# New hand-set first steps, fewer warming products and a new written order in a clustered-attention and two-MLP kernel

## The chip, the cores and the metric

The kernel runs on one core of a Trainium2 chip. The metric is the device time of one execution in microseconds (us); a comparison uses the median of several executions. The core has five engines that work side by side: TensorE (PE, matrix products; its weight loads are shown as PEld), VectorE (DVE), ScalarE (ACT), GpSimd (POOL) and SyncE (SP, which here only issues DMA transfers).

## What is computed

Attention with 2 batches, 8 heads, 768 tokens and 64 channels per head, in which a query sees only the keys of its own cluster; then two MLPs on the 1536 tokens of 512 channels.

```
q_assign = argmax(q_n @ c_n.T);  k_assign = argmax(k_n @ c_n.T)   # 16 centroids per head
mask   = q_assign[:, None] == k_assign[None, :]
attn   = softmax(where(mask, q @ k.T / 8, -1e9));  x = attn @ v
h      = x @ w_in                                   # 512 -> 2048
x      = where(h > 0, h, exp(min(h, 0)) - 1) @ w_out
out    = ((x @ w_a) * (x @ w_b)) @ w_out2           # 512 -> 1536 -> 512
```

Weights come as 64-bit floats. Results are float32; every factor of a product is split into a high and a low part, so that one product becomes several.

## The kernel before, in words

The work is cut into 16 heads (`g`), taken two at a time as 8 pairs (`j`). A head's scores are 6 tiles (`t`) of 128 queries by 768 keys; three tiles make a half (`f`).

No loop orders the work. A long string, `ORDER`, lists some 2300 words, and the last loop of the kernel calls one small function for each. A word such as `th:0.1.1.0/pt=0` is a name, its numbers, and the buffer to take. Every engine runs its own instructions in the order of the words, and waits where an operand or a buffer is not ready. Where a function has a choice of engine, the last number makes it: 0 is DVE, 1 is ACT, 2 is POOL (for loads, 0 is SP's queue and 1 ACT's).

The words of the attention, by what they do:

- Loads: `lk` keys and `lp` queries of a pair, `lq` one head's queries twice (two transfers), `vl` a quarter of V, `wl` a piece of a weight; `kbd`, `ohd` are copies by DMA between tiles.
- Clusters: `c0` to `c4` prepare the centroids (a square root by ACT in `c1`, a transposition by PE in `c3`), `sm` is 24 cluster products of a pair, `m1` to `m5` the argmax on DVE (a one-hot result), `oh`, `ohs`, `ohd` bring it as 16 further rows into the operands; `ot`, `oe` do so for the first pair without a DMA (`oe:0`, `oe:1` on DVE, `oe:2`, `oe:3` on ACT).
- Operands: `qa`, `ka1`, `kb` are the high parts, `qb`, `ka2` the low parts.
- A tile: `sc` scores (4 products, two PSUM buffers), `rm` row maximum on DVE, `ex` exponential on ACT. Then it is transposed in one of two ways. By PE: `tr` transposes half a tile, `th` copies its high part (DVE or ACT), `tl` subtracts the low part on DVE. By DMA: `hi` and `lo` split it in float16 (ACT, POOL or DVE), `td` is the transposing transfer.
- V: `vr` the absolute maximum of a head (ACT, 16 of them), `vtp`, `vtd`, `vbp`, `vbd` turn these into scales, `vs` scales, `v1`, `v2` split.
- Results: `av` products with V in three parts, `ra`, `rc`, `rx`, `rb`, `re` the reciprocal of the row sums spread over the channels, `ev` the result.
- `wm` is a group of 8 products of zeros, whose result nobody reads. `cs` and `ce` are one-element activations, for square root and exponential; `cz`, `md`, `mo`, `sb` set constants on POOL; `ib` copies an identity matrix on DVE; `cE`, `cA`, `cB`, `cP` hand memory on.

Weights are converted piece by piece (`wl`, `wa`, `w0` to `w4`, `wh`, `ws`, `wq`) on ACT, DVE and POOL while PE works. The MLPs follow as `h`, `r1`, `r2`, `g`, `gh`, `gl`, `x2`, `xa` and `ab`, `bs`, `pr`, `ph`, `pl`, `o`, `oa`; `xh` and `xl` split their input. The first words of the MLPs stand among the last ones of the attention.

Of the kernel before, what the change touches and what calls it, by code (L numbers as in the profile page):

```python
# [70 lines left out]
m1:0/mx=0 m2:0 wh:0 vr:12 vr:15 wm:30 w3:0 wm:31 wm:56 w4:0 m3:0 vr:5 wm:40 vr:6 vr:4 wm:13  # L71
lq:3.0/rawq=1 m4:0 vr:7 wm:45 wm:16 wl:1 wm:1 ka1:2.1 m5:0/oht=0 ot:1/tt=2 wm:39 ws:0 vr:0 oe:1 vr:3
vr:1 vr:2 ka2:2.2 ot:2/tt=0 wm:18 ot:0/tt=1 wm:58 vtp:0/tt=2 oe:2 oe:0 qa:3.1 wm:8 wm:3 sc:0.0/sc=0
vtd:0 wq:0 wm:47 sc:0.1/sc=1 vbp:0/tt=0 ot:3/tt=1 wm:41 ka2:3.2 wa:1 rm:0.0/nm=0 qa:2.1
ex:0.0/pf=0/sum=0 wm:52 qb:2.0 lp:1.0/rawp=1 vbd:0 sc:0.2/sc=0 rm:0.1/nm=1 vs:2 oe:3 tr:0.0.0/tt=2
wm:51 ex:0.1/pf=1 wm:21 lk:2.0/rawk=0 tr:0.0.1/tt=0 rm:0.2/nm=2 tr:0.1.0/tt=1 ex:0.2/pf=2
# [12 lines left out]
rx:0.0/rx=0 tl:0.4.1 th:1.3.1.0/pt=3 ka2:4.2 tl:1.3.1 wa:2 vs:4 ka2:5.2 av:0.0.1 rb:0.0/tt=0
sc:2.0/sc=0 ex:1.5/pf=1 ra:0.1/rs=1 hi:1.5.1/phl=1 re:0.0.0/rb=0 tr:1.3.0/tt=1 lo:1.4.2 rm:2.0/nm=0  # L90
lq:5.0/rawq=1 rc:0.1 tl:0.4.0 ex:2.0/pf=0/sum=0 sc:2.1/sc=1 av:0.0.2 lp:3.0/rawp=1 tr:2.0.0/tt=0
th:1.3.0.1 rm:2.1/nm=1 sc:2.2/sc=0 tl:1.3.0 v2:3.2/v2=2 ex:2.1/pf=2 qa:5.1 sc:3.0/sc=1 ev:0.0
lo:1.5.2 th:2.0.0.1/pt=0 rm:2.2/nm=2 rx:0.1/rx=1 ex:2.2/pf=1 rb:0.1/tt=2 tr:2.0.1/tt=1 td:0.5
th:2.0.1.1 w0:2 sc:3.1/sc=0 rm:3.0/nm=3 re:0.1.1/rb=1 ex:3.0/pf=0 v2:2.2/v2=3 tl:2.0.0 tl:2.0.1
td:1.4 tr:2.1.1/tt=2 rm:3.1/nm=0 tr:2.1.0/tt=0 hi:2.2.2/phl=2 th:2.1.1.1 tr:3.0.0/tt=1 tl:2.1.1
ex:3.1/pf=2 sc:3.2/sc=1 sc:2.3/sc=0 hi:3.1.1/phl=3 lo:2.2.2 qb:5.0 w1:2 lo:3.1.2 rm:3.2/nm=1
th:3.0.0.1/pt=1 rm:2.3/nm=2 td:1.5 w2:2 sm:2/tt=2 th:2.1.0.1 w3:2 ex:3.2/pf=1 w4:2 td:2.2
lq:7.0/rawq=1 ex:2.3/pf=2/sum=1 hi:3.2.1/phl=0 sc:2.5/sc=1 ra:1.0/rs=0 lo:3.2.2 m1:2/mx=0
sc:2.4/sc=0 rm:2.4/nm=3 tl:2.1.0 wh:2 m2:2 ka1:6.1 m3:2 qa:6.1 ws:2 av:0.1.0 rm:2.5/nm=0 av:0.1.1
m4:2 wq:2 ex:2.4/pf=1 rc:1.0 tr:3.0.1/tt=0 th:3.0.1.1 wl:3 sc:3.3/sc=0 hi:2.4.1/phl=1 m5:2/oht=0  # L100
ex:2.5/pf=0 av:0.1.2 tl:3.0.0 oh:2/tt=2 tr:2.3.1/tt=1 wa:3 lo:2.4.2 td:3.1 rm:3.3/nm=1 ev:0.1
sc:3.5/sc=1 ohs:2/ohs=1 th:2.3.1.0/pt=2 ex:3.3/pf=1 tr:2.3.0/tt=2 sc:3.4/sc=0 tl:3.0.1 ka2:6.2
rm:3.5/nm=2 rx:1.0/rx=0 hi:2.5.1/phl=2 td:3.2 th:2.3.0.1 rb:1.0/tt=0 qa:7.1 lo:2.5.2 ex:3.5/pf=2
tl:2.3.1 rm:3.4/nm=3 w0:3 av:1.0.0 ohd:2 td:2.4 lk:4.0/rawk=0 av:1.0.1 tr:3.3.1/tt=1 qb:7.0 ka1:7.1
re:1.0.0/rb=0 ex:3.4/pf=0 hi:3.5.1/phl=3 sc:4.0/sc=1 tr:3.3.0/tt=0 tl:2.3.0 th:3.3.1.1/pt=3
rm:4.0/nm=0 kbd:5 ka2:7.2 th:3.3.0.1 tl:3.3.1 ex:4.0/pf=1/sum=0 sc:4.1/sc=0 hi:3.4.1/phl=0 av:1.0.2
# [12 lines left out]
th:4.3.0.0/pt=2 ka2:8.2 tr:5.3.1/tt=0 ka1:9.1 th:4.3.1.1 av:2.0.0 rm:5.5/nm=3 ex:5.4/pf=2 tl:4.3.0
av:2.0.1 qa:9.1 hi:5.4.1/phl=1 ka2:9.0 tr:5.3.0/tt=2 qb:8.0 ohd:3 qb:9.0 tl:4.3.1 ex:5.5/pf=0  # L120
th:5.3.0.1/pt=3 sc:6.0/sc=1 av:2.0.2 hi:5.5.1/phl=0 th:5.3.1.1 sc:6.1/sc=0 lo:5.4.2 rm:6.0/nm=0
tl:5.3.0 ex:6.0/pf=2/sum=0 rb:2.0/tt=1 sc:6.2/sc=1 tl:5.3.1 re:2.0.1/rb=0 rm:6.1/nm=1 td:4.4
lo:4.5.2 ev:2.0 ra:2.1/rs=1 lo:5.5.2 ex:6.1/pf=1 tr:6.0.0/tt=2 sc:7.1/sc=0 th:6.0.0.1/pt=0 td:5.4
tr:6.0.1/tt=0 rm:6.2/nm=2 ex:6.2/pf=0 th:6.0.1.1 tr:6.1.1/tt=1 hi:6.2.1/phl=3 w3:3 vs:12 tl:6.0.0
# [1034 lines left out]
```

## Time and profile before

| | |
|---|---|
| median of 3 runs | 803.97 us (801.41 to 805.08) |
| the profiled execution | 803.56 us, of which 801.8 us are its span |
| PE busy | 786.2 us (98%) |
| DVE busy | 580.0 us (72%) |
| ACT busy | 414.1 us (52%) |
| POOL busy | 355.5 us (44%) |
| mean granted clock of PE | 0.994 of full speed |

The span goes from the first to the last instruction. Busy shares are averages over an attention part and an MLP part of different kind. Matmuls are pipelined and their recorded ends are modelled, so a busy PE is not a PE at its peak.

### The profile page before, as it was taken

What the parts mean: (1) busy time and instruction counts of PE and PEld (TensorE: products, weight loads), DVE (VectorE), ACT (ScalarE), POOL (GpSimd) and SP (SyncE); (2) the same over time, 40 slices, a digit from 0 to 9 for tenths busy, and PEclk for the clock granted to TensorE, in tenths of its full rate; (3) what the DMA queues carried; (4) which work ended last, traced back from release to release, by engine and by line L of the source; (5) the groups of instructions that cost most, each with busy time, mean ns of one, the idle gap of its engine ahead of it and who ended that gap; (6) DMA issues with size and microseconds to landing.
All of it is one profiled execution on the core that took longest, in us unless ns stands there. A gap on an engine that the chain in (4) does not pass through costs nothing.

```text
span 801.8 us, 11888 instructions
## 1 busy us (share of the span) xinstructions
PE 786.2 (98%) x4474; PEld 645.2 (80%) x4474; DVE 580.0 (72%) x838; ACT 414.1 (52%) x717; POOL 355.5 (44%) x290
## 2 busy tenths in 40 slices
...
GB/s 311 156 170 165 204 153 202 217 187 159 158 120 46 60 53 105 75 84 104 78 56 105 80 78 27 81 77 54 1 53 76 79 57 52 53 54 0 53 1 105
DMA packets 98009, 79.12 MB, mean 99 GB/s; under 512 B 81248, under 2 KB 81248, under 8 KB 97952
## 3 DMA queue, kind: packets, MB, share of 16 engines
...
q10 hardware_dynamic: 304, 0.79, 0.3%
...
## 4 chain that ended last, share of the span: by engine, by line
PE 82%; issue 5%; DVE 4%; ACT 3%; DMA 3%; POOL 2%; SPq 1%; POOLq 0%; ACTq 0%; DVEq 0%
PE ab L942 8%; PE ab L943 8%; PE ab L941 8%; PE sc L689 6%; PE x L941 5%; PE h L941 5%; PE h L943 5%; PE x L943 5%; PE h L942 5%; PE x L942 5%; PE o L942 4%; PE o L943 4%; PE o L941 4%; PE av L802 4%; PE tt L743 2%
## 5 line engine op out<-in xcount | busy, mean ns | idle before, releaser
L697 DVE TENSOR_REDUCE nm<-sc 128x1 f32<-128x768 f32 x96 | 90.6, 949 | 6.8 <-PE sc L689 6.3
L725 POOL TENSOR_TENSOR phl<-pf,phl 128x768 f16<-128x768 f32 x49 | 84.2, 1723 | 22.1 <-ACT phl L718 12.7
L710 ACT ACTIVATE pf<-sc,nm 128x768 f32<-128x768 f32 x96 | 86.9, 905 | 10.1 <-DVE nm L697 7.2
L1043 ACT COPY t0ab<-ab 128x512 f32<-128x512 f32 x36 | 21.1, 587 | 109.2 <-PE ab L943 109.2
L1048 DVE TENSOR_TENSOR t1ab<-ab,t0ab 128x512 f32<-128x512 f32 x36 | 24.8, 689 | 63.2 <-ACT t0ab L1043 63.2
L689 PE MATMUL sc<-ka,qa 128*128 128x384 f32 x192 | 59.3, 391 | 4.3 <-ACT pf L710 3.8
L872 ACT ACTIVATE wg<-wraw 128x512 f32<-128x512 f32 x68 | 45.0, 667 | 26.8 <-DMA wraw<-in_w_out_dram 14.4
L802 PE MATMUL av<-pt,v 128*64 128x384 f16 x576 | 54.9, 334 | 0.6 <-DMA qb<-ohs 0.6
L889 DVE SCALAR_TENSOR_TENSOR wf<-wraw,wg 128x512 int32<-128x512 int32 x68 | 51.5, 760 | 1.8
L689 PE MATMUL sc<-kb,qb 80*128 80x384 f32 x192 | 51.0, 347 | 0.4 <-DMA kb<-ka 0.4
L752 DVE TENSOR_TENSOR pt<-tt,pt 128x384 f16<-128x384 f32 x92 | 48.6, 544 | 2.5 <-ACT pt L747 2.3
L902 DVE SCALAR_TENSOR_TENSOR wg<-wraw,wg 128x512 f32<-128x512 uint32 x68 | 49.2, 724 | 1.5
L1059 DVE TENSOR_TENSOR gl<-t1ab,gh 128x512 fp32r<-128x512 f32 x36 | 33.9, 941 | 18.7 <-ACT gh L1054 18.5
L743 PE MATMUL tt<-identf,pf 128*128 128x128 f32 x276 | 44.2, 281 | 2.9 <-DVE pt L752 2.6
L802 PEld LDWEIGHTS <-v 128*64 128x64 f16 x576 | 31.2, 111 | 19.0 <-issue 8.0
L877 DVE TENSOR_SCALAR wg<-wg 128x512 f32<-128x512 f32 x68 | 39.3, 578 | 8.1 <-ACT wg L872 8.0
L689 PEld LDWEIGHTS sc<-ka,qa 128*128 128x128 f32 x192 | 30.1, 195 | 14.5 <-ACT pf L710 11.8
L743 PEld LDWEIGHTS tt<-identf,pf 128*128 128x128 f32 x276 | 32.3, 143 | 11.6 <-DVE pt L752 2.0
L882 DVE TENSOR_SCALAR wg<-wg 128x512 int32<-128x512 int32 x68 | 38.4, 566 | 1.8
L1005 ACT CAST gh<-t1h 128x1024 fp32r<-128x1024 f32 x24 | 25.2, 1052 | 27.6 <-DVE t1h L997 27.6
L997 DVE SCALAR_TENSOR_TENSOR t1h<-t0h,h 128x1024 f32<-128x1024 f32 x24 | 29.2, 1216 | 13.1 <-ACT t0h L992 13.1
L1099 DVE TENSOR_TENSOR acc<-o,acc 128x1024 f32<-128x1024 f32 (+1 forms) x12 | 14.2, 1180 | 32.3 <-PE o L943 32.3
...
## 6 DMA issues: line engine op xcount, KB each, us to landing
...
acc<-in_v_dram SPq DMA_DIRECT2D x4, 768.0 KB, 11.0
...
```

The source lines that it names most:

```text
L689: nc.tensor.matmul(s[:, j, :HALF], a[:, qs], b[:, j * HALF : (j + 1) * HALF], start=i == 0, stop=i == 1,)
L697: nc.vector.reduce_max(out=nm, in_=st[g][f"sc{t}"][:, :, :HALF], axis=AX.XY, negate=True)
L710: nc.scalar.activation(pf.rearrange("p (a b) -> p a b", a=2), st[g].pop(f"sc{t}")[:, :, :HALF], AF.Exp, bias=st[g].pop(f"nm{t}"), accum_ou ...
L725: (nc.vector, None, nc.gpsimd)[e].tensor_sub(phl[:, S:], st[g].pop(f"pf{t}"), phl[:, :S])
L743: nc.tensor.transpose(tt[:, k * P : (k + 1) * P], pf[:, o : o + P], identf)
L752: nc.vector.tensor_sub(lo, st[g].pop(f"tt{t}{u}"), hi)
L802: nc.tensor.matmul(pairs[j]["av"][x * 64 : (x + 1) * 64].rearrange("p (a q) -> p a q", a=3), st[2 * j + x][("v1", "v2")[vi]][:, kt_, :], s ...
L889: nc.vector.scalar_tensor_tensor(out=f, in0=raws[n][:, :, 1], scalar=-0x40000000, in1=g, op0=ALU.bitwise_and, op1=ALU.bitwise_or,)
L902: nc.vector.scalar_tensor_tensor(out=g, in0=raws.pop(n)[:, :, 0].bitcast(U32), scalar=2.0 ** -52, in1=g, op0=ALU.mult, op1=ALU.mult,)
L941: nc.tensor.matmul(ps, lhi, rhi, start=first, stop=False)
L942: nc.tensor.matmul(ps, lhi, rlo, start=False, stop=False)
L943: nc.tensor.matmul(ps, llo, rhi, start=False, stop=last)
```

## The change

Only the string `ORDER` differs; every function stays. The words up to the first MLP block are written anew, and the words from `h:1.0.1` on are the same.

- The words of the start stand in a new sequence. The centroids' steps (`c0` to `c4`), the first pair's cluster products and its argmax come first; `wl:0` and two quarters of V are issued ahead of the other queries; head 0's queries come by ACT's queue and head 1's by SP's, the other way round than before. The maxima `vr` stand among the first scores and exponentials, where before all 16 stood ahead of them.
- `wm` appears 12 times, before 60 times. Before the first score (`sc:0.0`) stand 7 of them, before 44.
- Engines: `th` 71 times on ACT and 21 on DVE (before 76 and 16); `hi` 41 on ACT and 9 on POOL (38 and 12); `lo` 47 on POOL and 3 on DVE (49 and 1); `qa` 11 on ACT and 5 on POOL (16 and 0); `ka1` 11 on ACT and 5 on POOL (13 and 3); `ka2` 13 on POOL and 3 on DVE (12 and 4); `re` 14 on ACT and 2 on DVE (12 and 4). Which heads and tiles these are changes too. `v1` keeps its counts (14 on ACT, 2 on POOL) for other heads; `ka2:0.0` and `qb` stay on DVE.
- The same 50 tiles are transposed by DMA and the same 46 by PE. All their steps stand in a new order, with other buffers.

The start of the string on both sides (the rest of some 150 lines is of the same kind):

```diff
 ORDER = """
-lk:0.1/rawk=0 wm:0 wm:2 lp:0.0/rawp=0 lq:1.1/rawq=0 cz:0 lq:0.0/rawq=1 ib:0 wm:4 wm:6 cs:0 wm:7
-wm:10 vl:2 wm:11 wl:0 mo:0 wm:15 kb:1 md:0 vl:3 wm:14 wm:19 ka1:0.1 vl:1 sb:0 wm:22 vl:0 ka1:1.1
-kb:0 wm:25 ka2:1.0 wm:27 wm:28 c0:0 c1:0 wm:29 wm:26 qa:1.1 wm:33 c2:0 qb:1.0 wm:37 qa:0.1 ka2:0.0
-wm:38 wm:5 wm:20 qb:0.0 lq:2.0/rawq=0 vr:9 vr:10 c3:0/tt=0 wm:46 vr:8 wm:48 c4:0 wm:24 wm:53 wm:55
-wm:17 wm:42 vr:11 wa:0 wm:49 w0:0 w1:0 vr:14 sm:0/tt=1 wm:57 wm:23 w2:0 vr:13 lk:1.0/rawk=1 ka1:3.2
...
+lk:0.1/rawk=0 lp:0.0/rawp=0 wm:0 wl:0 lq:0.1/rawq=0 c0:0 vl:0 c1:0 cz:0 c2:0 wm:2 vl:1 c3:0/tt=0
+ka1:0.1 c4:0 sm:0/tt=1 lq:1.0/rawq=1 cs:0 wa:0 kb:1 ka2:0.0 ib:0 qa:0.2 md:0 kb:0 ka1:1.2 m1:0/mx=0
+ka2:1.2 m2:0 m3:0 wm:4 m4:0 ce:0 wm:6 wm:7 wm:10 m5:0/oht=0 ot:2/tt=2 oe:2 qb:0.0 ot:0/tt=0 vr:0
+w0:0 oe:0 w1:0 vr:1 vl:2 vr:2 wm:11 ot:3/tt=1 sc:0.0/sc=0 sc:0.1/sc=1 w2:0 qa:1.2 rm:0.0/nm=0
+lk:1.0/rawk=1 wm:15 oe:3 ot:1/tt=2 vr:3 vr:4 rm:0.1/nm=1 ex:0.0/pf=0/sum=0 tr:0.0.0/tt=0 vr:5 w3:0
+wm:14 oe:1 qb:1.0 w4:0 ex:0.1/pf=1 vl:3 tr:0.1.1/tt=1 lq:2.0/rawq=0 wm:19 vr:6 tr:0.1.0/tt=2 vr:7
+vr:8 wm:22 vr:9 vr:10 vr:11 sc:0.2/sc=0 th:0.1.1.0/pt=0 lq:3.0/rawq=1 tl:0.1.1 vr:12 ka1:2.2 ka1:3.2
+vr:13 vr:14 vr:15 th:0.1.0.0 ka2:2.2 lp:1.0/rawp=1 wh:0 mo:0 wm:25 wl:1 rm:0.2/nm=2 sb:0 ws:0
+sc:1.0/sc=1 lk:2.0/rawk=0 wq:0 th:0.0.0.0 rm:1.0/nm=3 tl:0.1.0 ex:0.2/pf=2 vtp:0/tt=1 sc:1.1/sc=0
...
```

## Rows read from the trace of the kernel before

**Rows 1.** Busy time of the engines by stretch, with instructions, clock and DMA.

```profile
0.00:45.00 45.00, 42.56 (x572) 40.23 (x573) 30.58 (x58) 35.45 (x77) 18.93 (x42) 1.00 0.73 223
45.00:236.40 191.40, 182.90 (x1401) 141.78 (x1401) 179.34 (x285) 175.74 (x354) 153.65 (x123) 0.97 0.89 175
236.40:802.00 565.60, 560.77 (x2505) 463.18 (x2503) 370.05 (x497) 202.94 (x289) 182.97 (x126) 1.00 0.20 63
```

The columns are: from and to, length, busy time of PE, PEld, DVE, ACT and POOL (us, with instructions), granted clock of PE, DMA share, GB/s.

**Rows 2.** Timeline of PE, the first MLP product: start, duration.

```profile
236.45 0.48 PE L941 MATMUL h<-x0h,w0h 128*128 128x512 f32 x1
```

**Rows 3.** Waits from 45 to 236 us: sum, times, longest.

```profile
DVE nm L697 <- PE sc L689: 5.6, 13, 1.2
ACT pf L710 <- DVE nm L697: 7.0, 12, 1.5
```

**Rows 4.** Timeline, 0 to 62 us; in brackets the idle time before.

```profile
7.57 0.23 DVE L371 TENSOR_TENSOR csq<-cn 128x64 f32<-128x64 f32 x1
12.51 0.46 DVE L401 COPY cblk<-cps 64x64 f32<-64x64 f32 x2 [0.54 <-PE cps L395]
18.66 0.56 DVE L616 TENSOR_REDUCE mx<-tp 128x24 f32<-128x384 f32 x1 [3.40 <-PE tp L602]
27.28 0.59 PE L689 MATMUL sc<-ka,qa 128*128 128x384 f32 x2
31.15 0.90 ACT L710 ACTIVATE pf<-sc,nm 128x768 f32<-128x768 f32 x1
54.47 0.90 ACT L710 ACTIVATE pf<-sc,nm 128x768 f32<-128x768 f32 x1 [1.48 <-DVE nm L697]
57.65 0.88 ACT L710 ACTIVATE pf<-sc,nm 128x768 f32<-128x768 f32 x1
```

**Rows 5.** Groups by line up to 236.4 us: busy us, mean ns.

```profile
L747 DVE CAST pt<-tt 128x384 f16<-128x384 f32 x15 | 8.2, 546 | 1.5 <-PE av L802 1.5
L747 ACT CAST pt<-tt 128x384 f16<-128x384 f32 x69 | 31.6, 480 | 0.5 <-PE tt L743 0.3
L718 ACT CAST phl<-pf 128x768 f16<-128x768 f32 x38 | 31.6, 832 | 0.3
L718 POOL CAST phl<-pf 128x768 f16<-128x768 f32 x12 | 11.9, 992 | 6.1 <-issue 2.9 <-ACT pf L710 2.8 <-POOL phl L725 0.4
L725 POOL TENSOR_TENSOR phl<-pf,phl 128x768 f16<-128x768 f32 x49 | 84.2, 1723 | 22.1 <-ACT phl L718 12.7 <-issue 8.3
L565 POOL TENSOR_TENSOR ka<-rawk,ka 64x768 fp32r<-64x768 f32 x12 | 22.2, 1849 | 4.2 <-ACT ka L558 3.4
L583 ACT ACTIVATE qa<-rawq 128x768 fp32r<-128x768 f32 x16 | 13.4, 843 | 0.0
```

**Rows 6.** Timeline of PE, 82 to 102 us.

```profile
95.82 0.60 PE L689 MATMUL sc<-ka,qa 128*128 128x384 f32 x2
...
96.61 0.82 PE L743 MATMUL tt<-identf,pf 128*128 128x128 f32 x3
97.08 0.99 PE L689 MATMUL sc<-ka,qa 128*128 128x384 f32 x2
...
98.64 1.83 PE L802 MATMUL av<-pt,v 128*64 128x384 f16 x12
```

**Rows 7.** Busy time by stretch, three short stretches, columns as above.

```profile
0.00:4.00 4.00, 2.80 (x27) 2.81 (x28) 1.05 (x3) 1.49 (x2) 1.72 (x28) 1.00 0.48 170
4.00:8.00 4.00, 4.00 (x71) 4.00 (x69) 1.35 (x3) 3.32 (x4) 0.00 (x0) 1.00 1.05 285
...
96.60:100.00 3.40, 3.40 (x18) 2.38 (x18) 2.76 (x5) 2.52 (x6) 3.10 (x3) 0.50 1.04 260
```

**Rows 8.** DMA issues up to 30 us: KB each, us to landing.

```profile
cn<-in_cent_dram SPq DMA_DIRECT2D x1, 32.0 KB, 3.4
```

**Rows 9.** Busy time of the line of `vr` alone, up to the first score.

```profile
0.00:27.28 27.28, 9.85 (x32) 1.00 0.89 292
```

**Rows 10.** The line of `qb`: duration least, median, most (ns), first and last start.

```profile
L508 DVE SCALAR_TENSOR_TENSOR qb<-rawq,qa x16: 940/951/2531, 9.1 to 192.1; 64x768 fp32r<-64x768 f32 x16
```

More of the change, by code (lines that the diff above doesn't have):

```diff
@@ L71 @@
[L71 to L76, printed above, removed]
@@ L89 @@
[L89 to L94, printed above, removed]
@@ L95 @@
[L95 to L106, printed above, removed]
@@ L119 @@
[L119 to L124, printed above, removed]
@@ new lines @@
+ohd:1 av:0.0.0 kbd:3 th:0.4.0.1 tl:0.4.1 av:0.0.1 th:1.3.1.1/pt=3 sc:2.0/sc=0 ex:1.4/pf=2 tl:0.4.0
+tl:1.3.1 tr:1.3.0/tt=1 ws:1 rx:0.0/rx=0 sc:2.1/sc=1 wq:1 v1:3.1/v1=3 ka2:4.0 hi:1.5.1/phl=0
+hi:1.4.1/phl=1 qb:4.0 ra:0.1/rs=1 av:0.0.2 rm:2.0/nm=0 ka1:5.1 th:1.3.0.1 ex:2.0/pf=0/sum=0
+sc:2.2/sc=0 lp:6.0/rawp=1 td:0.5 tr:2.0.1/tt=0 rm:2.1/nm=1 lo:1.4.2 tl:1.3.0 kbd:5 wa:2 v2:3.2/v2=2
+lo:1.5.0 ex:2.1/pf=2 rb:0.0/tt=2 sc:3.0/sc=1 th:2.0.1.1/pt=0 re:0.0.1/rb=0 tr:2.1.0/tt=1
+lq:5.0/rawq=1 tr:2.1.1/tt=2 td:1.4 rm:2.2/nm=2 rc:0.1 tl:2.0.1 ka2:5.2 ex:2.2/pf=1 th:2.1.1.1
@@ new lines @@
+sc:5.5/sc=0 lq:9.0/rawq=0 th:4.3.1.1/pt=2 tl:5.0.0 lk:5.0/rawk=1 v1:7.1/v1=1 ka2:8.2 td:5.1
+rm:5.4/nm=2 tl:4.3.1 hi:4.5.1/phl=0 rm:5.5/nm=3 qa:9.2 td:5.2 tr:5.3.1/tt=2 lp:4.0/rawp=0 w3:3
+av:2.0.0 tr:5.3.0/tt=0 ex:5.4/pf=1 av:2.0.1 ohd:3 td:4.4 hi:5.4.1/phl=3 th:5.3.0.1/pt=3 kbd:7
+ex:5.5/pf=2 sc:6.0/sc=1 sc:6.1/sc=0 qb:8.0 ra:2.1/rs=1 qb:9.0 lo:5.4.2 tl:5.3.0 rm:6.0/nm=0 td:5.4
+rb:2.0/tt=0 th:4.3.0.1 lo:4.5.2 av:2.0.2 tl:4.3.0 rm:6.1/nm=1 th:5.3.1.1 ex:6.0/pf=1/sum=0 rc:2.1
+w4:3 sc:6.2/sc=1 kbd:8 vs:14 hi:5.5.1/phl=2 rm:6.2/nm=2 re:2.0.1/rb=0 ex:6.1/pf=0 tr:6.0.0/tt=1
@@ new lines @@
+m4:4 ex:6.3/pf=1/sum=1 th:7.0.1.1/pt=1 v2:6.2/v2=3 sc:6.5/sc=1 rc:3.0 ex:6.4/pf=2 m5:4/oht=0
+hi:6.4.1/phl=2 oh:4/tt=1 th:7.0.0.1 lo:7.2.2 tl:7.0.1 sc:7.3/sc=0 av:2.1.2 tr:6.3.1/tt=0 rm:6.5/nm=0
+tl:7.0.0 ohs:4/ohs=1 ex:6.5/pf=0 rx:3.0/rx=0 wl:4 rm:7.3/nm=1 lq:10.0/rawq=1 lq:11.0/rawq=0 lo:6.4.2
+ka1:10.2 ev:2.1 ex:7.3/pf=2 tr:6.3.0/tt=2 sc:7.5/sc=1 hi:6.5.1/phl=1 th:6.3.1.0/pt=2 ka2:10.2 td:7.1
+qa:10.1 th:6.3.0.0 rm:7.5/nm=2 tr:7.3.0/tt=1 tl:6.3.0 lo:6.5.2 td:7.2 sc:7.4/sc=0 av:3.0.0 ohd:4
+tr:7.3.1/tt=2 lp:5.0/rawp=0 td:6.4 rm:7.4/nm=3 tl:6.3.1 ex:7.5/pf=1 ka1:11.1 th:7.3.1.0/pt=3 qa:11.1
@@ new lines @@
+tl:9.0.1 td:7.5 sc:8.3/sc=1 hi:9.1.1/phl=1 ra:3.1/rs=1 rm:9.2/nm=1 lo:8.2.2 lo:9.1.2 vs:10
+th:8.1.1.1 wa:4 ex:9.2/pf=1 sm:5/tt=0 rm:8.3/nm=2 ev:3.0 v2:9.2/v2=0 ex:8.3/pf=2/sum=1 tl:8.1.1
+rc:3.1 rx:3.1/rx=1 sc:8.4/sc=0 m1:5/mx=1 hi:9.2.1/phl=3 v1:8.1/v1=2 lk:6.0/rawk=0 sc:8.5/sc=1
+v2:8.2/v2=1 lq:12.0/rawq=0 av:3.1.0 m2:5 kbd:11 lo:9.2.2 td:8.2 rm:8.4/nm=3 av:3.1.1 m3:5 th:9.0.0.1
+rb:3.1/tt=1 td:9.1 rm:8.5/nm=0 qa:12.2 lq:13.0/rawq=1 ra:4.0/rs=0 ka1:12.1 ex:8.4/pf=0 m4:5
+m5:5/oht=1 hi:8.4.1/phl=0 lo:8.4.2 tl:9.0.0 td:9.2 sc:9.3/sc=0 ex:8.5/pf=1 oh:5/tt=0 tr:8.3.1/tt=2
```

225 lines of the change are left out of this document (112 added, 113 removed).

## Prediction

> **What bounds the kernel now.** I read the stages first: busy time of each engine in the attention's start, its middle and everything behind the first MLP product [rows 1]. Behind 236.4 us TensorE (PE) is busy for 560.8 of 565.6 us. The first MLP product starts at 236.45 [rows 2], so those 565 us are the MLPs at PE's own pace; the order of its steps is the same in both kernels but for a few dozen words at the transition. The change can act on one number only: when PE reaches the first MLP product.
>
> Ahead of it VectorE (DVE) and ScalarE (ACT) are both nearly full. From 45 to 236.4 us DVE works 179.3 of 191.4 us and ACT 175.7 [rows 1]. Next I read who waits for whom in that stretch. All waits of DVE come to 10.7 us in this view; its longest entry is the row maximum waiting for a score (5.6 us in 13 waits), and ACT's longest is the exponential waiting for that maximum (7.0 us in 12) [rows 3]. So the two hand work to each other with little slack: extra work on either is paid about half, and a wait is paid fully. PE's 182.9 us there are no sign of a bound, since its matmuls overlap in the records. GpSimd (POOL) has 153.7 us.
>
> Last I read the start in order of time [rows 4]. The first score runs at 27.28 us and the first exponential at 31.15. Up to 45 us DVE works 30.6 us and ACT 35.5 [rows 1], so DVE has 14.4 us idle and ACT 9.5. That idle time is what hand-set first steps can take.
>
> **The start.** The chain to the first score is: centroids, block descriptor, cluster products (`sm:0`), argmax (`m1` to `m5`), one-hot rows (`ot`, `oe`), score. In the kernel before, its first DVE step stands behind a subtraction and runs at 7.57 us; it ends at 12.97 (12.51 + 0.46) with 2.85 us of other DVE work between, so by itself it takes 2.55 us [rows 4]. After the change it waits only for the centroids, issued at 0.75 and landing 3.4 us later [rows 8]. It can thus run from 4.2 to 6.9 us (an estimate with 0.15 for hand-overs).
>
> `sm:0` then takes 2.65 us at full clock (the 24 products of 15.81 to 18.46, seen as 3.40 us of wait ahead of the first maximum [rows 4]). At half clock I take 1.56/0.79 as long, 5.2 us: from the first product of a score to its successor on PE it is 0.79 us at 95.82 and 1.56 at 97.08 [rows 6], where the granted clock is 0.50, the 1.2 GHz level [rows 7]. The argmax is five steps, 3.1 us with gaps. One more group of products and ACT's first one-hot copy (`oe:2`) follows at 13.4 us; at half clock it is 16.5, since four warming groups (32 products) stand ahead of it as well. DVE needs `qb:0.0` and `oe:0` (0.95 each) behind that, so the first score starts at about 15.3, or 18.2, against 27.28.
>
> Those 9 to 12 us are not all kept. In the kernel before, ACT spends the early time on the sixteen maxima of V (`vr`, 9.85 us in all [rows 9]) and has them all behind it at the first exponential. Now 3 of 16 stand ahead of the first score and 11 stand between the first and the third exponential. I therefore count ACT's work up to the point where pair 1's first score (`sc:2.0`) stands in the order: from `oe:2` on 37.3 us (40.5 less 3.2 done sooner; each step by its row, an exponential as 1.0). That gives 50.7 or 53.8 us. The kernel before has 2.7 us of ACT waits between its first exponential and this point, 1.48 of it at 54.47 [rows 4]; I leave these in, since nothing in the words removes them: 53.4 or 56.5. The kernel before is there at 57.65. The start thus gives back 4.2 us at full clock, 1.1 at half; between the two, **-2.6 us**. DVE's own work up to there (38.6 us from 4.2, 10 us of idle) ends at about the same time, so it does not decide.
>
> **Loads.** V's first quarter has 2.4 MB queued up to its end and its last 5.5 MB. By the DMA rate of 285 GB/s [rows 7] they land near 10 and 20 us; `vr:0` and `vr:12` come at 14 and 25 us or later. The keys and queries of pair 1 stand behind `qb:0.0` and `qb:1.0` on SP's queue and are wanted ten microseconds later. Cost nothing, with these margins as cover. If a load is late, ACT stands behind it in order, for at most the lateness.
>
> **Fewer warming products.** 48 groups of 8 go, 384 products of 56 ns (71 products in 4 us [rows 7]), 21.6 us of PE. Before the first score, 44 groups become 7, where PE had nothing else to do; behind it 16 become 5, 4.9 us of PE less while pair 0 runs. PE hides either, so no gain is counted. Their cost is the clock: the first 4 us hold 27 products in 2.80 us of busy time, 104 ns each, and the next 4 us have 56 ns, though the clock column, which has no record that early, reads 1.00 [rows 7]. So the array starts at the 1.2 GHz level and steady products raised it. That is why both clocks stand in the sum above. The Trainium skill ("TensorE: Matmul & The Clock Gate", section "What's actually happening") says that the default state is throttled and that activity releases it; the first 8 us agree. By that rule the start gives 1.1 us and the total is 1.5 us later than mine.
>
> **Casts and copies on other engines.** Counted from the words, priced from [rows 5]. ACT loses five `th` (0.480), two `ka1` (0.83, as the cast of equal length) and five `qa` (0.843), and gains three `hi` (0.832) and two `re` (0.48): -2.4 - 1.7 - 4.2 + 2.5 + 1.0 = -4.8 us. DVE gains five `th` (0.546) and two `lo` and loses one `ka2` (0.95 each, as `qb`, which has two inputs of equal length [rows 10]) and two `re` (0.55): +2.7 + 1.9 - 0.9 - 1.1 = +2.6. POOL gains two `ka1` and five `qa`, loses three `hi` (0.992) and two `lo` (1.723), gains one `ka2` (1.849). No `qa` runs on POOL in the trace: it lies between a cast of its shape (0.992) and a two-input step (1.723), nearer the cast, which also has one input; +2.0 in all, to +5.7 at most.
>
> Most of ACT's relief falls into the start and is counted there. Behind `sc:2.0` the words leave ACT as much work as before, DVE 3.8 us more and POOL 6.9 more. As the two engines share the bound, half of DVE's counts: **+1.9** (nothing if ACT decides throughout, 3.8 if DVE does). POOL's share is hidden in its 38 us of idle time between 45 and 236.
>
> POOL can also slow DVE: `qb` takes 0.951 us in the median and 2.531 at worst [rows 10]. One such step costs 1.6 us, and 6.9 us more work on POOL's 154 should add no further one to sixteen; I count none and allow a few in the range. The Trainium skill ("GPSIMD Engine Reference", section "Key points") says that POOL shares its SBUF interfaces with DVE and contends with instructions of two SBUF inputs. The slow `qb` agrees; by that rule all of POOL's extra time overlapping such steps would cost some microseconds, in the direction of slower.
>
> **The new order.** It deals DVE's 10.7 us of waits anew. Scores wait for exponentials to free their two buffers, so where ACT is relieved the 5.6 us of waits for scores should shrink; I take about half, **-2.5**. Nothing in the words excludes all of them going, or as many new ones.
>
> **Sum.** -2.6 + 1.9 - 2.5 = -3.2. The profiled execution took 803.56 us (span 801.8, 1.8 around it), 0.4 under the median of 803.97. 803.56 - 3.2 = 800.4, with the median's offset 800.5.
>
> **Rivals.** (1) *The order removes nearly all the waits.* Then -10.7 in place of -2.5, and the start at full clock gives 4.2: 803.6 - 4.2 + 1.9 - 10.7 = 790.6; with the start as forecast 792. For it: DVE and ACT wait for each other only, and only order sets that. Against it: both are 92% busy or more, and steps with three hand-overs rarely fit without a gap.
>
> (2) *Slower: the clock stays at 1.2 GHz through pair 0.* A tile then costs PE 1.56 for the score, about 1.0 for two transposes and 0.4 as share of `sm:1`, 3.0 us, where ACT takes 2.41 ((57.65 - 31.15)/11 [rows 4]). PE becomes the bound: 12 tiles by 0.6 are 7 us, and the start gives 1.1 only: -3.2 + 1.5 + 7 = +5.3, 808.9. It decides from where the granted clock is half for more than about 8 tiles. The page named above would lead there too, if activity fell too low (the Trainium skill, "TensorE: Matmul & The Clock Gate", section "What's actually happening"). For it: at 96.6 us the clock fell right behind a burst of cluster products [rows 6, 7] in a stretch without warming. Against it: PE slowed to the bound is busy all the time, and the steady products at the start raised it.
>
> (3) *Nothing comes of the earlier start.* ACT's V maxima and DVE's extra work take it all: -1.1 + 3.8 - 2.5 = 0, 804.
>
> **How the numbers follow.** The bound for a real difference is 0.5%, 4 us. The forecast has 0.40, its own range is 797.5 to 804; a third of it (0.13) lies below 800. Rival 1 has 0.27, rival 2 0.20, rival 3 0.13. Faster 0.13 + 0.27 = 0.40; same 0.27 + 0.13 = 0.40; slower 0.20. The range goes from 791 (rival 1) to 808 (nearly rival 2).
>
> **What would show it.** The first score between 15 and 19 us, the first exponential between 18 and 22, `sc:2.0` 1 to 4 us ahead of 57; the first MLP product near 233; DVE waits between 45 us and there of about 8 us. The granted clock in the first 40 us tells rival 2; waits of DVE under 4 us tell rival 1. The forecast is wrong if the first MLP product moves by over 4 us beyond what the start gave, or if PE has gaps behind it, which I took as unchanged.

## The result and the profile after

The changed kernel takes 807.55 us (median of 20, 803.24 to 813.34), the kernel before 803.81 (median of 20, 800.32 to 805.58): a ratio of 1.0058, 95% interval 1.0037 to 1.0079. The ratio lies above the 0.5% that the prediction counts as a difference, though its interval reaches below it. 807.55 lies in the range given (791 to 808), at the end that came from rival 2; the forecast of 800.5 had the sign wrong.

The profile at hand is of the execution of 813.34 us, the longest of the 20. A second one, of an execution of 806.81 us, comes with the experiments and is nearer to the median. First the stages, to be set against [rows 1], and 33.0 to 56.9 us by itself:

```profile
0.00:45.00 45.00, 35.15 (x224) 31.73 (x225) 30.50 (x58) 30.46 (x68) 20.50 (x43) 0.83 0.72 206
45.00:247.50 202.50, 189.79 (x1369) 148.44 (x1368) 182.00 (x288) 178.41 (x359) 157.76 (x125) 0.91 0.86 168
247.50:811.50 564.00, 560.17 (x2502) 462.99 (x2500) 371.02 (x498) 201.56 (x285) 182.38 (x126) 1.00 0.19 63
33.00:56.90 23.90, 20.12 (x79) 17.93 (x78) 17.82 (x29) 17.03 (x33) 14.08 (x13) 0.50 0.61 118
```

The timeline's first MLP product, to be set against [rows 2]:

```profile
247.51 0.49 PE L938 MATMUL h<-x0h,w0h 128*128 128x512 f32 x1
```

Behind it stand 564.0 us, 1.3 fewer than before (801.8 - 236.45 = 565.35): the loss lies wholly ahead of the first MLP product. There the granted clock has fallen, and from 33.0 to 56.9 us it is 0.50, the 1.2 GHz level, where the kernel before has 1.00 up to 57.65. The waits from 45 us to the first MLP product answer to [rows 3]:

```profile
DVE nm L694 <- PE sc L686: 14.0, 22, 2.4
ACT pt L744 <- PE tt L740: 6.6, 9, 3.0
ACT pf L707 <- DVE nm L694: 5.2, 7, 1.7
```

VectorE's (DVE's) waits for scores have grown from 5.6 to 14.0 us, where the prediction had them shrink; ScalarE (ACT) waits for transposes, which was not among its longest waits before. Both wait for TensorE (PE). All of VectorE's waits in this stretch come to 19.4 us, where the prediction had about 8 for 10.7 before. Last the start, against [rows 4]:

```profile
3.59 0.23 DVE L368 TENSOR_TENSOR csq<-cn 128x64 f32<-128x64 f32 x1 [2.46 <-DMA cn<-in_cent_dram]
5.72 0.46 DVE L398 COPY cblk<-cps 64x64 f32<-64x64 f32 x2 [0.71 <-PE cps L392]
11.61 0.56 DVE L613 TENSOR_REDUCE mx<-tp 128x24 f32<-128x384 f32 x1 [4.33 <-PE tp L599]
17.12 0.62 PE L686 MATMUL sc<-ka,qa 128*128 128x384 f32 x2
20.61 0.90 ACT L707 ACTIVATE pf<-sc,nm 128x768 f32<-128x768 f32 x1
...
52.71 0.96 DVE L694 TENSOR_REDUCE nm<-sc 128x1 f32<-128x768 f32 x1 [0.74 <-PE sc L686]
...
58.02 0.92 ACT L707 ACTIVATE pf<-sc,nm 128x768 f32<-128x768 f32 x1
```

The first score is 10.2 us ahead and the first exponential 10.5 ahead of before. The 58.02 is the twelfth exponential, the counterpart of the 57.65 in [rows 4]: the lead is gone, and 0.4 us more.

### The profile page after: what moved, and what is told of

Same layout as the page of the kernel before. It is cut to its first block, busy times and chain, and to the rows that moved or that the text cites. A ratio compares the mean times of both kernels' runs of the same rounds, so it can differ in the third digit from the quotient of the medians.

```text
span 811.5 us, 11114 instructions
## 1 busy us (share of the span) xinstructions
PE 785.1 (97%) x4090; PEld 643.2 (79%) x4090; DVE 583.5 (72%) x842; ACT 410.4 (51%) x710; POOL 360.6 (44%) x293
## 4 chain that ended last, share of the span: by engine, by line
PE 84%; ACT 8%; issue 3%; DVE 2%; DMA 2%; POOL 1%; SPq 0%; ACTq 0%; DVEq 0%; POOLq 0%
PE ab L938 8%; PE ab L939 8%; PE ab L940 8%; PE sc L686 6%; PE h L938 5%; PE h L939 5%; PE x L939 5%; PE h L940 5%; PE x L940 5%; PE x L938 5%; PE o L938 4%; PE o L940 4%; PE o L939 4%; PE av L799 3%; ACT pf L707 3%; PE tt L740 3%
## 5 line engine op out<-in xcount | busy, mean ns | idle before, releaser
L722 POOL TENSOR_TENSOR phl<-pf,phl 128x768 f16<-128x768 f32 x47 | 79.7, 1700 | 34.8 <-ACT phl L715 30.6
L686 PE MATMUL sc<-ka,qa 128*128 128x384 f32 x192 | 63.1, 412 | 10.4 <-ACT pf L707 9.9
L799 PE MATMUL av<-pt,v 128*64 128x384 f16 x576 | 56.8, 340 | 0.0
L686 PE MATMUL sc<-kb,qb 80*128 80x384 f32 x192 | 54.3, 366 | 1.1 <-DMA kb<-ka 1.1
L686 PEld LDWEIGHTS sc<-ka,qa 128*128 128x128 f32 x192 | 32.4, 209 | 23.3 <-ACT pf L707 20.0
L740 PE MATMUL tt<-identf,pf 128*128 128x128 f32 x276 | 46.7, 295 | 3.4 <-ACT pf L707 2.8
L740 PEld LDWEIGHTS tt<-identf,pf 128*128 128x128 f32 x276 | 35.5, 151 | 11.2 <-ACT pf L707 3.6
L686 PEld LDWEIGHTS sc<-kb,qb 80*128 80x128 f32 x192 | 39.0, 210 | 1.3 <-issue 1.3
L1096 DVE TENSOR_TENSOR acc<-o,acc 128x1024 f32<-128x1024 f32 (+1 forms) x12 | 14.2, 1180 | 32.3 <-PE o L940 32.3
```

Source lines behind the costliest of these rows:

```text
L686: nc.tensor.matmul(s[:, j, :HALF], a[:, qs], b[:, j * HALF : (j + 1) * HALF], start=i == 0, stop=i == 1,)
L722: (nc.vector, None, nc.gpsimd)[e].tensor_sub(phl[:, S:], st[g].pop(f"pf{t}"), phl[:, :S])
L740: nc.tensor.transpose(tt[:, k * P : (k + 1) * P], pf[:, o : o + P], identf)
L799: nc.tensor.matmul(pairs[j]["av"][x * 64 : (x + 1) * 64].rearrange("p (a q) -> p a q", a=3), st[2 * j + x][("v1", "v2")[vi]][:, kt_, :], s ...
```

## The experiments

Each kernel was compared with the kernel before on the same chip; several chips were used, so the ratios are what to compare. "First MLP" is its start in the one profiled execution. The expectations test theories: the clock theory, C, puts the loss down to TensorE's half clock in pair 0; the order theory, O, to the new order behind the start; the engine theory to the engine moves; W to VectorE's added work, with the start's lead only work put off.

| kernel | warming groups | median us | ratio, 95% | first MLP |
|---|---|---|---|---|
| after, again (e12) | 12 | 809.41 | 1.0071, 1.0040 to 1.0102 | 240.95 |
| e1 | 24 | 805.13 | 1.0024, 1.0002 to 1.0046 | 238.08 |
| e13 | 12, later | 808.07 | 1.0056, 1.0025 to 1.0087 | 241.05 |
| e14 | 33 | 807.37 | 1.0041, 1.0010 to 1.0071 | 239.50 |
| e9 | 45 | 803.31 | 1.0010, 0.9983 to 1.0036 | 235.52 |
| e16, e9 again | 45 | 807.10 | 1.0057, 1.0025 to 1.0089 | 240.55 |
| e2, before | 12 | 802.97 | 0.9991, 0.9970 to 1.0012 | 236.18 |
| e17, before, 7 casts on DVE | 60 | 807.48 | 1.0057, 1.0035 to 1.0080 | 238.87 |

**Where the time goes: the changed kernel again.** No edit.

> The changed kernel once more, unchanged, for a second profile: the one at hand is of an execution of 813.3 us, the longest of 20, whose median is 807.5. Every theory: 806 to 809. Theory C: fewer and shorter stretches at half clock than the 51 us in the profile at hand, the one of 33 to 57 us among them again. Theory W: VectorE's work ahead of the first MLP product 212 to 213 us again, its idle time 4 to 6 us less than the 35.0 of that profile.

To read a profile as a sum I cut the time ahead of the first MLP product at the 12th, 24th, 48th and 72nd exponential, which mark the same progress of the softmax in every kernel. In each line VectorE's idle time is the length less its busy time, the third after the length. First the kernel before, then e12:

```profile
0.00:57.65 57.65, 53.68 (x673) 49.26 (x674) 42.36 (x76) 46.00 (x96) 29.16 (x50) 1.00 0.73 211
57.65:82.86 25.21, 23.87 (x183) 17.45 (x181) 24.29 (x41) 24.59 (x49) 20.17 (x16) 1.00 0.78 166
82.86:137.76 54.90, 51.90 (x370) 40.52 (x370) 49.10 (x78) 49.30 (x99) 43.15 (x37) 0.94 0.98 186
137.76:188.42 50.66, 48.74 (x380) 38.00 (x374) 47.87 (x75) 46.51 (x97) 43.66 (x34) 0.97 0.98 198
188.42:236.45 48.03, 47.32 (x380) 36.83 (x376) 46.35 (x77) 44.85 (x94) 36.44 (x30) 1.00 0.79 144
```

```profile
0.00:58.21 58.21, 44.80 (x271) 38.99 (x273) 40.68 (x75) 40.52 (x89) 30.25 (x50) 0.77 0.64 183
58.21:88.94 30.73, 27.95 (x202) 21.44 (x198) 27.67 (x45) 27.42 (x55) 20.81 (x16) 0.89 0.94 190
88.94:138.47 49.53, 47.95 (x369) 37.59 (x368) 47.79 (x78) 48.09 (x95) 45.41 (x37) 1.00 1.02 205
138.47:191.49 53.02, 48.27 (x367) 37.56 (x365) 48.51 (x73) 46.19 (x93) 44.58 (x33) 0.97 0.91 187
191.49:240.95 49.46, 48.83 (x393) 38.25 (x391) 47.11 (x79) 46.83 (x99) 39.12 (x32) 1.00 0.76 137
```

VectorE's idle times are 15.3, 0.9, 5.8, 2.8, 1.7 us before (26.5) and 17.5, 3.1, 1.7, 4.5, 2.4 in e12 (29.2); its work is 210.0 and 211.8. Three things stand in these lines. Up to the 12th exponential VectorE has done 1.7 us less in e12 (40.68 for 42.36): part of the early scores is work put off, which the second stretch makes up (27.67 for 24.29). The first two stretches hold 4.4 us more idle time, at clocks of 0.77 and 0.89. And from the 24th to the 48th the new order does what the prediction hoped of it: 4.1 us less idle time. By theory W the 211.8 is as expected within 0.3, and the idle time is 5.8 us under that of the long execution. The median of 809.41 lies just above the 806 to 809 that every theory had.

**Warming behind the scores (e1).** In the changed kernel one more group behind each of the 12 scores of pair 0:

```diff
-sc:0.0/sc=0 sc:0.1/sc=1 w2:0
+sc:0.0/sc=0 wm:60 sc:0.1/sc=1 wm:61 w2:0
```

> The changed kernel with one group of 8 warming products more behind each of the 12 scores of pair 0 (24 groups in all, 17 of them behind the first score, where the kernel before has 16). Clock theory (the loss is the 1.2 GHz stretches that fewer warming products leave): the granted clock stays at full speed from 20 to 65 us, the first MLP product moves from 247.5 to about 238, and the time falls from 807.5 to 797 to 800. Order theory (the loss lies in the new order and the engine moves): the time stays within 2 us of 807.5, or grows by the 5 us of added products.

The ratio fell from 1.0058 to 1.0024: what clock is given back is worth some 2.7 us by these two numbers, whose intervals overlap, and some loss stays. 805.13 fits neither theory: the clock theory had at most 800, the order theory at least 805.5.

**45 groups, twice (e9, e16).** On top of e1's, one more group behind each of TensorE's remaining steps ahead of the first AV product, 21 in all:

```diff
-rm:0.0/nm=0 lk:1.0/rawk=1 wm:15 oe:3 ot:1/tt=2 vr:3
+rm:0.0/nm=0 lk:1.0/rawk=1 wm:15 oe:3 ot:1/tt=2 wm:12 vr:3
```

> The changed kernel with 45 warming groups: those of e1_warm_back and one more behind every other step of TensorE's ahead of the first AV product (transposes of the exponentials, mask products). Theory C (the half clock of pair 0 is the loss): the granted clock of the first 60 us rises from 0.76 (0.94 in e1_warm_back) to 0.97 or more, first MLP product at 236 to 237, 802 to 804, ratio 0.999 to 1.002. Theory W (what is left in e1_warm_back is VectorE's work, 2.6 us more, and the start's lead is work put off): no better than e1_warm_back, 804 to 806, ratio 1.001 to 1.005. If the extra products stand in the way of the scores, later than e1_warm_back.

> e9_warm_45 once more, unchanged, because its ratio (1.0010) stands beside 1.0041 and 1.0047 of the two kernels built on it. If the clock of pair 0 is all of the loss: 0.999 to 1.002 again. If it is about half of it, and the rest is VectorE's added work and the new order behind pair 0: 1.002 to 1.005, 804.5 to 807.

The first stretches of e9, cut as above, then those of e16:

```profile
0.00:56.01 56.01, 49.26 (x527) 44.60 (x529) 40.18 (x75) 40.44 (x88) 30.79 (x50) 1.00 0.67 194
56.01:85.48 29.47, 25.89 (x210) 20.07 (x205) 28.54 (x44) 27.27 (x55) 21.08 (x16) 1.00 0.98 203
85.48:135.02 49.54, 48.29 (x374) 37.91 (x374) 48.35 (x80) 48.09 (x95) 45.41 (x37) 1.00 1.02 201
135.02:186.05 51.03, 48.20 (x362) 37.63 (x360) 48.15 (x72) 46.18 (x94) 44.29 (x33) 0.97 0.92 193
```

```profile
0.00:55.93 55.93, 49.18 (x527) 44.52 (x529) 40.17 (x75) 40.45 (x88) 30.78 (x50) 1.00 0.68 194
55.93:83.88 27.95, 25.66 (x210) 19.79 (x205) 27.02 (x44) 27.24 (x54) 20.83 (x16) 1.00 1.01 202
83.88:136.67 52.79, 51.46 (x374) 39.71 (x374) 48.39 (x80) 48.52 (x95) 45.43 (x37) 0.94 0.98 194
136.67:191.11 54.44, 49.34 (x363) 38.41 (x362) 48.91 (x72) 46.14 (x93) 43.89 (x33) 0.94 0.92 182
```

In both the clock is 1.00 through the first two stretches, and VectorE's idle time there is 16.8 and 16.7 us for 20.6 in e12: with the half clock of pair 0 gone, 3.8 us less are lost at that place, in both profiles. Two kernels further down hold the same words up to there. e15 idles 16.2 us at a clock of 1.00, but in e18 45 groups did not hold the clock, and it idles 21.6:

```profile
0.00:58.83 58.83, 51.39 (x527) 46.38 (x529) 41.86 (x75) 40.43 (x88) 30.31 (x50) 0.97 0.63 184
58.83:91.17 32.34, 30.15 (x210) 24.14 (x205) 27.67 (x44) 27.43 (x54) 20.82 (x16) 0.84 0.89 176
```

VectorE's waits for scores up to its 12th exponential in e9 and in e12:

```profile
DVE nm L688 <- PE sc L680: 2.8, 5, 1.1
```

```profile
DVE nm L694 <- PE sc L686: 4.6, 4, 3.0
```

But e16 then loses 5.9 us more idle time than e9 from the 24th to the 72nd (4.4 and 5.5 us for 1.2 and 2.9), at a clock of 0.94 twice. It is the same program, and the two comparisons gave 1.0010 and 1.0057. The 803.31 was partly luck.

**The same 12 later, and 33 (e13, e14).** e13 moves the 12 groups behind the 12 scores; e14 takes the 12 original groups out of e9.

```diff
-ot:3/tt=1 sc:0.0/sc=0 sc:0.1/sc=1 w2:0
+ot:3/tt=1 sc:0.0/sc=0 wm:0 sc:0.1/sc=1 wm:2 w2:0
```

> The changed kernel with the same number of warming groups, 12, but one behind each of the 12 scores of pair 0 and none ahead of the first score. Theory C with the place deciding: the clock of 33 to 57 us stays up, 804 to 806, ratio 1.000 to 1.003, though the mask products at the start run at half clock. Theory C with the number deciding (only more products of any place help): as the changed kernel, 806.5 to 809, ratio 1.004 to 1.008.

> e9_warm_45 without the 12 groups that the changed kernel has: 33 groups, five of them ahead of the first score. If the place decides: as e9_warm_45, 802.5 to 804.5, ratio 0.998 to 1.002. If the number decides: between e1_warm_back (24 groups, 805.1) and e9_warm_45 (45, 803.3): 804 to 805, ratio 1.001 to 1.003.

The first two stretches of e13, then of e14:

```profile
0.00:54.77 54.77, 37.82 (x273) 31.74 (x275) 39.98 (x74) 40.38 (x89) 30.25 (x50) 0.94 0.69 194
54.77:85.52 30.75, 27.77 (x200) 21.22 (x196) 27.72 (x45) 27.42 (x54) 21.61 (x17) 0.89 0.91 191
```

```profile
0.00:57.60 57.60, 43.92 (x431) 38.78 (x433) 41.63 (x75) 40.43 (x89) 29.67 (x50) 1.00 0.68 188
57.60:85.58 27.98, 25.12 (x201) 19.66 (x198) 27.05 (x44) 27.26 (x55) 21.40 (x16) 1.00 0.98 200
```

The place matters for the clock: with the same 12 groups it is 0.94 instead of 0.77 up to the 12th exponential, which comes 3.4 us sooner (behind it 0.89, as in e12). The time does not follow: 1.0056, as the changed kernel. e14 at 1.0041 answers neither of its two readings, though its clock is 1.00 in both stretches. So, with e14 and e16, an intact clock in pair 0 does not by itself bring the time of before back.

**The kernel before with 12 groups (e2).** The same 12 that the change keeps, nothing else.

```diff
-ka2:1.0 wm:27 wm:28 c0:0 c1:0 wm:29 wm:26 qa:1.1 wm:33 c2:0
+ka2:1.0 c0:0 c1:0 qa:1.1 c2:0
```

> The kernel before with the same 12 warming groups that the change keeps, the other 48 taken out, all else as before. Clock theory: granted clock at half in parts of the first 80 us, 4 to 10 us slower than before (808 to 814). Order theory: within 2 us of 803.8, since no other step changes and PE is not the bound.

```profile
0.00:60.70 60.70, 45.77 (x291) 40.49 (x292) 41.92 (x76) 46.27 (x96) 28.99 (x50) 0.72 0.67 193
60.70:85.90 25.20, 23.65 (x181) 17.37 (x180) 24.10 (x40) 24.58 (x49) 20.16 (x16) 1.00 0.90 183
...
0.00:236.18 236.18, 214.33 (x1588) 170.70 (x1589) 207.46 (x342) 211.78 (x430) 173.01 (x164) 0.92 0.88 184
```

Here too the clock falls (0.72) and the 12th exponential is 3.1 us late; yet the first MLP product is not, and the ratio is 0.9991, far from the 808 to 814 us of the clock theory: in the old order the 48 groups cost nothing to leave out. In this profile VectorE's steps took 2.5 us less in all (207.46 for 209.97, the same 342 instructions), and 1.4 us of idle time went behind the 24th exponential. Why the loss comes back in the old order is not shown.

**Order and engines apart (e3, e4).** e3 has the new order with every step on its engine of before, e4 the old order with the new engines. For example, in e3:

```diff
-hi:2.2.1/phl=2
+hi:2.2.2/phl=2
```

> The changed kernel with the engine of every cast and copy as in the kernel before (th, hi, lo, qa, ka1, ka2, v1, re and the two first loads), order and warming as changed. Clock theory: 807 within 3 us, since the clock is as poor as in the changed kernel. Engine theory (the 3.8 us of extra DVE work and 6.9 us of extra POOL work behind the start cost the time): 803 to 805.

> The kernel before with the changed kernel's engine for every cast and copy, order and 60 warming groups as before. Clock theory: 804 within 2 us. Engine theory: 806 to 808.

827.8 us (1.0311, 1.0280 to 1.0342) and 824.2 (1.0257, 1.0229 to 1.0285), with the first MLP product at 265.53 and 257.48: each is over 20 us slower, beyond every theory. Order and engines belong together, and the change cannot be split into an order's price and a price for the moves by such swaps.

**Added work of VectorE by itself (e17).** In the kernel before, seven casts of transposes (units 4, 5, 6, 7, 9) go from ScalarE to VectorE, as in the change:

```diff
-rc:1.1 th:4.0.0.1/pt=0 rx:1.1/rx=1
+rc:1.1 th:4.0.0.0/pt=0 rx:1.1/rx=1
```

> The kernel before with seven casts of transposes in units 4 to 9 moved from ScalarE to VectorE, as the change does, and nothing else: VectorE's work 3.8 us more (546 ns each), ScalarE's 3.4 us less. The prediction counts half of such work: 804.5 to 805, ratio 1.002 to 1.003. If VectorE decides throughout: 806.5, ratio 1.0045. If only the balance of the two matters: 802 to 803.5, ratio 0.999 to 1.001.

807.48 for 803.37 us: 4.1 us (2.8 to 6.4 by the interval) for 3.8 us of work. It is paid in full, not by half.

**Work taken off again (e10, e15, e18).** e10 and e15 put five casts of e1 and of e9 back on ScalarE, e18 puts three `qa` of e9 back from GpSimd (POOL) on ScalarE:

```diff
-th:6.3.1.0/pt=2 ka2:10.2 td:7.1
+th:6.3.1.1/pt=2 ka2:10.2 td:7.1
...
-rm:5.5/nm=3 qa:9.2 td:5.2
+rm:5.5/nm=3 qa:9.1 td:5.2
```

> e1_warm_back with five casts of transposes to f16 behind pair 2 (units 6, 8, 9, 10) moved from VectorE back to ScalarE, where the kernel before has four of them: 2.7 us less on VectorE (543 ns each), 2.4 us more on ScalarE, which stands idle 29 us ahead of the first MLP product. Theory W (VectorE sets the end, so its added work counts in full): first MLP product 1.5 to 2.7 us ahead of e1_warm_back's, 802.4 to 803.6, ratio 0.999 to 1.001. Theory C: as e1_warm_back, 804.5 to 806.

> e9_warm_45 with the five casts of e10_five_casts_on_act back on ScalarE: VectorE's work 2 to 2.7 us less. On e1_warm_back this gave 0.4 us of the first MLP product and 0.0002 of the ratio. If VectorE's work sets the end once the clock is up: 801 to 802, ratio 0.996 to 0.998, ahead of both kernels. If the relief turns into waits of VectorE for ScalarE, as it did on e1_warm_back: 803 to 804, ratio 0.999 to 1.002.

> e9_warm_45 with the three scaled queries of pairs 9, 12 and 13 back from GpSimd to ScalarE, where the kernel before has them: GpSimd's work 6.4 us less (2131 ns each), ScalarE's 2.5 us more. If GpSimd's load lengthens VectorE's steps that run beside it and delays the splits that scores wait for: 1 to 2 us faster than e16_warm_45_again, VectorE's work 0.5 to 1.5 us less. If GpSimd's load is hidden, as the prediction has it: the same as e16_warm_45_again, or slower by up to 1 us, since ScalarE has more to do.

Ratios of 1.0026 (1.0002 to 1.0049) beside e1's 1.0024, and 1.0047 (1.0020 to 1.0074) beside e9's 1.0010 and e16's 1.0057: the relief bought nothing that can be measured. e10's VectorE works 1.9 us less than e1's (212.16 for 214.09) and idles 1.6 more: the work taken off became waits. In e15's profile VectorE does not even work less than in e9's (214.02 us for 212.32), where 2 to 2.7 us less was expected. e18 with 804.47, 1.0030 (1.0001 to 1.0060) lies between e9 and e16 and settles nothing.

**Halves joined (h1, h2, h3, h5).** h1 takes the changed kernel's words up to `sc:2.0` and then what is left in the order of before, h2 the same with e1's start; h3 and h5 take the kernel before up to `sc:4.0` and up to `sm:6`, and then what is left in the new order. Where they join, h3 looks like this:

```diff
 ... hi:3.5.1/phl=3 (words of the kernel before, up to the first score of pair 2)
-sc:4.0/sc=1 tr:3.3.0/tt=0 tl:2.3.0 th:3.3.1.1/pt=3 ...
+ce:0 lp:6.0/rawp=0 kbd:5 lq:8.0/rawq=1 vs:11 tr:3.3.0/tt=0 tl:2.3.0 th:3.3.0.1/pt=3 tl:3.3.0 sc:4.0/sc=1 w1:3
 ... (what is left, as in the changed kernel)
```

> The changed kernel's words up to the first score of pair 1 (sc:2.0), with its 12 warming groups and its engine choices there; from there every word that is left, in the order and with the engines of the kernel before. Theory O (the loss comes from the new order behind sc:2.0): the twelfth exponential at 57 to 58 us as in both kernels, because the half clock of 33 to 57 us eats the early start, and the rest as before: 802 to 804 us, ratio 0.998 to 1.002. Theory C (the loss is the clock that the missing warming products leave at half speed): this kernel has the same start, so it carries the same loss: 806 to 808, ratio 1.004 to 1.007.

> As h1_start_of_after, but the start is that of e1_warm_back: one more warming group behind each of the 12 scores of pair 0, 24 in all. Theory O: the twelfth exponential at 54.7 us, 2.9 ahead of before, and nothing lost behind it: 799.5 to 801, ratio 0.996 to 0.998, faster than both kernels. Theory C: the clock is whole again, so this too is as before less the early start, 799.5 to 801; what tells O and C apart is h1 and h3. If the lead of 2.9 us is taken up by waits behind sc:2.0 whatever the order there, 802 to 804.

> The other way round: the kernel before up to the first score of pair 2 (sc:4.0), with all its warming products; from there the words that are left in the order and with the engines of the changed kernel. Theory O: 1 to 3 us are lost between exponentials 24 and 84 (e1_warm_back loses 3.0 of 3.0 us of its lead by the first MLP product): 804 to 807, ratio 1.002 to 1.005. Theory C: nothing lost, 802 to 804, ratio 0.998 to 1.002.

> The kernel before up to sm:6, some two thirds into attention; the rest in the order and with the engines of the changed kernel. Theory O with the loss at the end (e1_warm_back takes 26.1 us for exponentials 72 to 84, before 23.1): 804.5 to 806.5, ratio 1.002 to 1.005. Theory O with the loss in pair 1, or theory C: 802 to 804, ratio 0.998 to 1.002.

h1 810.64 (1.0107, 1.0066 to 1.0148), h2 808.47 (1.0075, 1.0049 to 1.0102), h3 805.47 (1.0049, 1.0024 to 1.0074), h5 804.07 (1.0013, 0.9987 to 1.0039). h1 and h2 missed both theories. VectorE idles 7.2 and 5.9 us behind the join up to the 24th exponential (32.95 - 25.79, 32.11 - 26.17), for 0.9 before and 3.1 in e12; that this is work which the new start had put off, coming in a heap, is my reading and not shown. They show that an early start and the old rest don't fit, not what the start is worth. h3 keeps the start of before, with its 60 groups and full clock, and still loses: some of the loss comes from the new rest. Its profile is of a long execution (809.62 us); there the 24th exponential comes at 83.32 us (82.86 before), and the idle time grows most from the 48th to the 72nd, 9.9 us for 2.8, at a clock of 0.85:

```profile
137.42:194.46 57.04, 53.45 (x362) 42.48 (x359) 47.18 (x72) 46.24 (x94) 43.92 (x33) 0.85 0.87 172
```

h5, with only the last third new, can't be told from no loss.

**The first steps alone (e11).** The changed kernel's first 50 words, then what is left of the kernel before, with all its warming groups.

```diff
 ... vl:2 vr:2 wm:11 ot:3/tt=1
-sc:0.0/sc=0 sc:0.1/sc=1 w2:0
+mo:0 wm:15 vl:3 wm:14 wm:19 sb:0 wm:22 ... (the order of before)
```

> The changed kernel's first 50 words alone (its first loads, constants and mask steps up to the first score), then the rest of the words of the kernel before in its order and with all 60 warming groups. The prediction has the gain of the start at 2.6 us: 800 to 801. Theory W: the mask work only trades places with loads and splits that VectorE does in that time anyway, 802 to 803.5, ratio 0.998 to 1.001.

810.0 us (1.0082, 1.0054 to 1.0111). The warming groups left over stand in a row ahead of the first score, and the first exponential came at 35.3 us instead of 31.15. So the edit delays the start instead of moving it ahead, and its result says nothing on the first steps.

## Why the prediction was wrong, point by point

**What bounds it: right.** Only the first MLP product's time matters. The part behind it was to stay as it was; it fell by 1.3 us.

**The start: the times right, their worth wrong.** First score between 15 and 19 us: 17.12; first exponential between 18 and 22: 20.61. The 12th exponential was to come between 53.4 and 56.5 for 57.65: 58.02 and 58.21 at half clock, 56.01 (e9) and 54.67 (e1) with the clock up for most of it. The mask products took as long as the lower case had it: 5.1 us (6.28 to 11.38), forecast 5.2. What failed is counting that lead as -2.6. Progress was read from ScalarE's exponentials; e9 is 1.6 us ahead at the 12th, but VectorE has done 2.2 us less by then (40.18 for 42.36). With the clock whole its idle time there is 15.8 us, for 15.3 before. e1 idles less up to there (14.2) at a clock of 0.94, but up to the 24th exponential e1, e9 and e16 have 15.4 to 16.8 us for 16.2 before: the start gains 0.8 us at most.

**Loads: right.** One transfer was late: ScalarE waited 4.0 us for a piece of a weight up to 9.1 us, and the first exponential still came within its range.

**Fewer warming products: this failed first.** Their products were rightly priced at nothing (e2 gains nothing without them), and the clock was named as their cost, but only up to the first score. Rival 2 had the case that came: half clock in pair 0. It was to decide from about 8 tiles on; the 23.9 us from 33.0 hold the exponentials 5 to 11, seven, and the score of the twelfth. Its argument against ("PE slowed to the bound is busy all the time") did not hold: from 33.0 to 56.9 us PE shows 20.12 us busy of 23.90, at half clock throughout. Its price was too high. From the third exponential (29.7 us) to the twelfth a tile takes 3.1 us, as forecast (3.0), but 2.9 in e9 with the clock up ((56.0 - 30.2)/9), where the rival took 2.41 from the order of before. So pair 0 and pair 1 lose 3.8 us, not 8.5. What is left of it at the end: the five kernels that differ from the changed one in warming alone (e1, e9, e16, e13, e14) have a mean ratio of 1.0038, the changed kernel in its two comparisons 1.0064; the difference is 0.0026, some 2 us, with single ratios spread from 1.0010 to 1.0057.

**Engine moves: counted right, weighed wrong.** VectorE was to have 2.6 us more up to the first MLP product: 212.51 for 209.97, +2.5. GpSimd was to have 2.0 to 5.7 more: 178.26 for 172.57, +5.7, and 180.17 in e12, +7.6, since a `qa` takes 2.13 us there, above both steps that it was put between. Five of sixteen `qb` are slow before and after (over 1.1 us, where the median is 0.95), so none was added, as forecast. VectorE's extra work behind `sc:2.0` was counted by half (+1.9 for 3.8); e17 has its price at 4.1 us for 3.8. That price is of the old order; in the new one taking casts off VectorE did not give time back (e10, e15).

**The new order's waits: the sign failed.** From -2.5 for waits that shrink to 14.0 us for 5.6 in the long execution, 7.6 in e12 and 5.4 in e9. The order does remove 4.1 us of idle time between exponentials 24 and 48 in e12, as rival 1 would have it everywhere; in that profile 1.7 are lost again up to the 72nd, 0.7 behind it, and 2.1 stand between the 12th and the 24th. In e16 only 1.4 of the gain is there.

**In place of -3.2** the runs show: next to nothing from the start; about 2 us from the clock of pair 0 (an estimate, from 0.3 to 4 us by the intervals of those seven comparisons); the remaining 0.0038, about 3 us, behind pair 0, in the new order with its moves, which h3 shows with an undisturbed start (1.0049). Its two candidates are VectorE's added work and TensorE's later stretches at half clock. A comparison of executions at the same mean clock, 0.992 to 0.995, on the same chip bears on them. There e9, e16 and e18 take 803.4, 803.7 and 803.1 us (means of 8, 2 and 5 executions), the kernel before 803.8 beside each: their loss stands in executions with a lower clock. e17 takes 807.5 for 803.8: its added work costs at the same clock. But e14 and e15, on another chip, take 805.6 and 807.1 for 803.6. So the two are not separated, this part stays open, and no version beats the kernel before.
